# Attention and two MLPs on one core: key loads ahead of the branch in a shared tile, weights decoded through PSUM in wider blocks, and a new schedule

## The chip, the cores and the metric

One NeuronCore of one Trainium2 chip runs the whole program. The metric is the device time of one execution in microseconds; the kernel before takes 1524.06 us (median of 3 runs, 1523.6 to 1525.9).

## What is computed

```python
# attention: q [1,12288,128], kv [1,384,32,128], w_sr [128,128]
kv_pool = kv.reshape(B, H//4, 4, W//4, 4, C).mean(axis=(2, 4))   # 768 keys, 16 rows each
k = v = kv_pool.reshape(B, -1, C) @ w_sr
s = scale * (q @ k.T); a = exp(s - s.max(-1)); a /= a.sum(-1) + 1e-9
x = a @ v                                    # tokens x 128
# first MLP (2048 wide)
x = relu(x @ w_in)**2 @ w_out
# second MLP (2048 wide): a rational function of h
h = x @ w_in
P = a0 + a1*h + a2*h**2 + a3*h**3
Q = 1 + |b0|*|h| + |b1|*h**2
out = (P / (Q + 1e-6)) @ w_out
```

The weights of the MLPs arrive as float64, two 32-bit words each.

## The kernel before

The tokens lie along the free dimension and are cut into blocks: one of 384, then blocks of 512, then 384 and 256. A float32 product on TensorE is done either as one fp32 product (two instructions) or as three fp32r products of a high and a low part (high x high, high x low, low x high).

Before anything else DVE computes some 25 small coefficients from the six numbers a and b, and a flag, which all engines read. `tc.If` then takes one of two bodies of the same `program`: SQUARES, where the polynomial can be completed to a square, or TERMS. The trace shows SQUARES (line 921 and 923 run), so TERMS is not spoken of.

A planner (`Plan`) gets every piece of work with a priority, the engines that may do it (each with a cost and a penalty added to the priority), what it reads and writes, and the ring of buffers (`bufs`) or the PSUM bank (`caps`, eight banks in all) that it needs. It simulates the engines and writes out one order; each engine executes its instructions in that order, and semaphores hold an instruction until its data and buffers are ready. The dictionary SQUARES holds ring sizes, penalties and offsets of the priorities.

The stages, with their lines:

- Start: 16 loads of 48 keys (384 KB each, line 448) into the ring `e` of five tiles; DVE sums each over 16 rows (452). TensorE multiplies the halves of the sums by w_sr for the keys (477) and the values (492); ACT and DVE split the results (481, 485, 504, 507, 511).
- Weights: `decode` (line 521 on) loads a piece of 256 columns as pairs of words into a slot of Z (531), POOL squares the high word as a float (538) for a test of magnitude, and DVE builds the float32 in four steps in a tile K in SBUF: shift (541), or (546), or (551), and a select and multiply (556). ACT and POOL then make the high (572, 598) and low parts (575, 601) where a weight is used split. There are 32 pieces: eight each for w_in and w_out of two MLPs.
- Attention, per tile of 128 tokens: scores (642), minimum of the negated scores on DVE (646), exponential on ACT (649), reciprocal on DVE (656, 657), scaling on POOL (660); then transpositions (683), copies out of PSUM (687 to 703), products with the values (712 to 716).
- First MLP, per block of 512 tokens 16 pieces of 128 hidden units: three fp32r products (768 to 770), relu on ACT (810) or DVE (813), square on ACT (816) or POOL (819); ten of 16 pieces are split into gH on ACT (828) and gL on POOL (834) for three products with w_out (786 to 788), six use fp32 (782).
- Second MLP, per block eight pairs of pieces (`G` = 2): products (768 to 770), |h| on ACT (907), the denominator either as a square on ACT (915) or, for the pairs in `qpool`, as two steps on POOL (910, 912); the completed square on ACT (921) and the cubic on DVE (923); logarithm and exponential on ACT (932, 933); division with one Newton step on DVE (945, 947, 950); then the product with w_out as fp32 (782), or, for the pairs in `spl`, split by a cast on ACT or DVE (960, 961) and a remainder on POOL (963) into three fp32r products.

The three MLP and attention stages of different blocks run at the same time: the first MLP about 17.5 sixteenths of a block ahead of the second, attention 18 more.

Of the kernel before, what the change touches and what calls it, by code (L numbers as in the profile page):

```python
# [10 lines left out]
F32 = mybir.dt.float32  # L11
# [33 lines left out]
    d2=3,  # L45
    g=2,
    pair=('kk', 'qp', 'sq2', 'ln', 'y0', 'g0', 'tt', 'rr', 'g2', 'ml'),
    rem=[],
    md_act=1,
    md_dve=0.5,  # L50
    rl_act=0.5,
    rl_dve=0,
    qh_act=8,
    qh_dve=0,
    spd=[],
    spl=[3],
    qpool=[0, 3, 4, 7],
    sq_act=2,
    sq_pool=4,
    gh_act=0,  # L60
    gh_dve=60,
    mh_act=4,
    mh_dve=8,
    ml_pool=0,
    ml_dve=60,
    ev_dve=0.5,
# [4 lines left out]
    warm=0,  # L71
# [3 lines left out]
        mh2=-245.5, mh1=-25.5, sc=-10.25, tr=0.5, nr=-177.0, g2=-51.5, ex=-83.25, kk=-203.75, rl=1.5, tt=11.75,  # L75
        ev=65.0, mo2=10.25, ln=64.75, g0=-54.25, ab=-12.0, sq=182.75, y0=-12.25, mn=-121.5, qp=23.75, av=-39.5,
        mo1=4.25, sP=113.25, sq2=158.25, rr=90.25, mh=-26.5, ml=-114.0,
# [10 lines left out]
    hs=[1, 4, 7],  # L88
    lo_dve=60.0,
    bufs=dict(  # L90
        qr=2, qh=2, ql=2, e=5, mn=4, sm=8, aT=2, xh=2, xl=2, yh=2, yl=2, aH=2, aL=2, g1=8, U=3, K=2,
        Z=8, o=1, gH=2, gL=2, mH=1, mL=1,
    ),
    caps=dict(
        h2=2, yb=2, sc=4, st=3, x=1, h1=2, y1=1, y2=1,
    ),
    lead1=22.5,
    leada=14.0,
    d1=5,
    d2=4,  # L100
    g=2,
    pair=('kk', 'qp', 'ln', 'y0', 'g0', 'tt', 'g2'),
    rem=[],
    md_act=0,
    md_dve=8,
    rl_act=0,
    rl_dve=8,
    qh_act=0,
    qh_dve=60,
# [3 lines left out]
    sq_act=0,  # L113
    sq_pool=0.5,
    gh_act=0,
    gh_dve=60.0,
    mh_act=0,
    mh_dve=60.0,
    ml_pool=0,
    ml_dve=60.0,  # L120
    ev_dve=60.0,
    hi_dve=60.0,
    rg=2,
    low=6,
# [5 lines left out]
        mh2=-10.75, mh1=-2.0, sc=-2.75, tr=-1.5, nr=-7.75, g2=0.5, ex=4.5, z2=6.0, t1=-1.0, kk=3.5, rl=-0.5,  # L130
        tt=6.75, ev=-1.75, mo2=5.75, ln=8.75, g0=10.0, ab=-2.0, sq=11.5, y0=-2.75, mn=1.25, qp=-6.5, av=0.5,
        mo1=0.75,
    ),
    free=150.0,
)
# [49 lines left out]
class Plan:  # L185


    def __init__(self, cfg, banks=8):
        bufs, caps = cfg["bufs"], cfg["caps"]
        self.cfg = cfg  # L190
        self.bufs = bufs
        self.banks = banks
        self.caps = caps
        self.slot = {}
        self.ops = []
        self.keys = {}
        self.seq = {}
# [939 lines left out]
```

## Time and profile before

| | |
|---|---|
| median of 3 runs | 1524.06 us |
| the profiled execution | 1524.5 us |
| its span, first to last instruction | 1522.7 us |
| TensorE (PE) busy | 1454.4 us, 96% |
| VectorE (DVE) | 1414.5 us, 93% |
| ScalarE (ACT) | 1407.9 us, 92% |
| GpSimd (POOL) | 1169.0 us, 77% |
| loaded from HBM | 21.04 MB |

All shares are over the whole span; the stages differ. PE busy time includes modelled ends of matmuls that overlap, so the mean duration of one is longer than the distance to the next. PEclk, the granted clock, is 1.00 at 2.4 GHz and 0.50 at 1.2 GHz.

### The profile page before, as it was taken

How to read it: one execution, taken by the hardware profiler on the slowest of the kernel's cores; microseconds unless marked ns; L12 is line 12 of the kernel's file. 1: busy time of each engine (PE TensorE's matmuls, PEld its weight loads, DVE VectorE, ACT ScalarE, POOL GpSimd, SP SyncE). 2: the span in 40 equal slices, each digit the busy share in tenths (PEclk: the TensorE clock that was granted, in tenths of full speed). 3: DMA queues.
4: the chain of work that ended last, by engine and by line, in shares of the span. 5: the costliest groups of instructions: out<-in, count | busy, mean ns of one | idle time of the engine just before them, and what ended most of it. 6: DMA issues, size and time to landing. Idle time of an engine off the chain costs nothing.

```text
span 1522.7 us, 18759 instructions
## 1 busy us (share of the span) xinstructions
PE 1454.4 (96%) x5893; PEld 1038.7 (68%) x5893; DVE 1414.5 (93%) x1892; ACT 1407.9 (92%) x2339; POOL 1169.0 (77%) x962
## 2 busy tenths in 40 slices
PE   2788999999999999999999999999999999999996
PEld 2666776676767766776777677677767677767764
DVE  6999899999999998989899999899999989999997
ACT  1676999999999999999999999999999999999996
POOL 1877887967879967877977878778768768778662
PEclk9999999999999999999999999999999999999997
DMA  6221000000000000000000000000000000000000
GB/s 234 77 77 42 1 13 8 7 15 8 8 8 15 8 8 14 2 13 8 15 8 8 14 8 8 15 8 8 15 7 8 8 13 4 8 8 1 8 8 12
DMA packets 16701, 28.62 MB, mean 19 GB/s; under 512 B 1872, under 2 KB 6864, under 8 KB 16592
## 3 DMA queue, kind: packets, MB, share of 16 engines
q1 hardware_dynamic: 16592, 27.34, 5.5%
q8 instruction: 48, 0.79, 0.2%
q14 instruction: 61, 0.50, 0.1%
HBM read 21.04 MB, written 6.29 MB: 18 GB/s over the span
## 4 chain that ended last, share of the span: by engine, by line
PE 81%; DVE 9%; ACT 3%; issue 2%; POOL 1%; DVEq 0%; ACTq 0%; POOLq 0%
PE psum L782 24%; PE psum L768 11%; PE psum L770 10%; PE psum L769 10%; PE psum L642 5%; PE psum L787 4%; PE psum L788 4%; PE psum L786 4%; PE psum L683 3%; PE psum L713 2%; PE psum L714 2%; PE psum L712 1%; DVE K L546 1%; PE psum L716 1%; DVE psum L947 1%
## 5 line engine op out<-in xcount | busy, mean ns | idle before, releaser
L834 POOL TENSOR_TENSOR gL<-g,gH 128x512 fp32r<-128x512 f32 (+2 forms) x250 | 312.4, 1260 | 79.1 <-ACT gH L828 33.0
L782 PE MATMUL psum<-Z,w1o 128*128 128x512 f32 (+2 forms) x700 | 330.6, 583 | 4.9 <-DVE Z L950 4.3
L819 POOL TENSOR_TENSOR g<-g 128x512 f32<-128x512 f32 (+2 forms) x281 | 282.2, 1020 | 28.5 <-ACT g L810 16.2
L923 DVE SCALAR_TENSOR_TENSOR Z<-Z,cf,psum 128x512 f32<-128x512 f32 (+2 forms) x400 | 280.4, 719 | 19.0 <-ACT Z L921 16.7
L921 ACT ACTIVATE Z<-psum,cf 128x512 f32<-128x512 f32 (+2 forms) x400 | 275.6, 726 | 0.0
L945 DVE SCALAR_TENSOR_TENSOR Z<-Z,v,psum 128x1024 f32<-128x1024 f32 (+2 forms) x200 | 246.0, 1233 | 28.0 <-ACT psum L933 25.9
L907 ACT ACTIVATE U<-psum 128x512 f32<-128x512 f32 (+2 forms) x400 | 236.3, 625 | 20.9 <-PE psum L770 17.0
L947 DVE SCALAR_TENSOR_TENSOR psum<-K,cf,psum 128x1024 f32<-128x1024 f32 (+2 forms) x200 | 247.3, 1237 | 0.0
L950 DVE SCALAR_TENSOR_TENSOR Z<-psum,Z 128x1024 f32<-128x1024 f32 (+2 forms) x200 | 234.8, 1174 | 2.5
L932 ACT ACTIVATE U<-K,cf 128x1024 f32<-128x1024 f32 (+2 forms) x200 | 233.5, 1170 | 1.5 <-POOL K L912 1.3
L912 POOL TENSOR_TENSOR K<-K,U 128x1024 f32<-128x1024 f32 (+2 forms) x100 | 231.2, 2312 | 4.0
L910 POOL TENSOR_SCALAR K<-U,cf 128x1024 f32<-128x1024 f32 (+2 forms) x100 | 109.3, 1093 | 138.4 <-ACT U L907 83.1
L933 ACT ACTIVATE psum<-U 128x1024 f32<-128x1024 f32 (+2 forms) x200 | 208.8, 1049 | 1.3 <-DVE Z L950 0.5
L768 PE MATMUL psum<-yh,w1h 128*128 128x512 f32 (+2 forms) x400 | 191.4, 479 | 4.2 <-DVE Z L950 1.5
L768 PE MATMUL psum<-xh,w0h 128*128 128x512 f32 (+2 forms) x400 | 185.6, 464 | 3.2 <-DVE Z L950 1.1
L782 PEld LDWEIGHTS psum<-Z,w1o 128*128 128x128 f32 x700 | 130.0, 192 | 80.2 <-issue 57.0
L828 ACT ACTIVATE gH<-g 128x512 fp32r<-128x512 f32 (+2 forms) x250 | 158.6, 671 | 0.3 <-PE psum L788 0.2
L810 ACT ACTIVATE g<-psum 128x512 f32<-128x512 f32 (+2 forms) x252 | 151.8, 633 | 3.2 <-PE psum L770 2.2
L770 PE MATMUL psum<-yh,w1l 128*128 128x512 f32 (+2 forms) x400 | 154.3, 386 | 0.0
L769 PE MATMUL psum<-yl,w1h 128*128 128x512 f32 (+2 forms) x400 | 153.9, 385 | 0.0
L770 PE MATMUL psum<-xh,w0l 128*128 128x512 f32 (+2 forms) x400 | 153.6, 384 | 0.0
L769 PE MATMUL psum<-xl,w0h 128*128 128x512 f32 (+2 forms) x400 | 153.0, 383 | 0.0
(123 smaller groups left out, 3107.4 us busy)
## 6 DMA issues: line engine op xcount, KB each, us to landing
e<-in_kv_dram SPq DMA_DIRECT2D x16, 384.0 KB, 4.5
qr<-in_q_dram SPq DMA_DIRECT2D x22, 256.0 KB, 2.6
out_dram<-o SPq DMA_DIRECT2D x22, 256.0 KB, 2.0
Z<-in_moe_w_in_dram SPq DMA_DIRECT2D x16, 256.0 KB, 3.1
Z<-in_moe_w_out_dram SPq DMA_DIRECT2D x16, 256.0 KB, 2.6
qr<-in_q_dram SPq DMA_DIRECT2D x2, 192.0 KB, 3.8
out_dram<-o SPq DMA_DIRECT2D x2, 192.0 KB, 1.9
qr<-in_q_dram SPq DMA_DIRECT2D x1, 128.0 KB, 2.0
```

The lines of the kernel that those rows point to most:

```text
L768: nc.tensor.matmul(out=out, lhsT=w_hi[m][:, sl], rhs=hi, start=True, stop=False)
L769: nc.tensor.matmul(out=out, lhsT=w_hi[m][:, sl], rhs=lo, start=False, stop=False)
L770: nc.tensor.matmul(out=out, lhsT=w_lo[m][:, sl], rhs=hi, start=False, stop=True)
L782: nc.tensor.matmul(out=o, lhsT=w_o[m][:, place[m][fi], :], rhs=rhs(), start=first, stop=last)
L819: nc.gpsimd.tensor_tensor(out=G(), in0=G(), in1=G(), op=ALU.mult)
L834: nc.gpsimd.tensor_tensor(out=mk("gL", gl)[:, :T], in0=G(), in1=f(tiles[gh][:, :T]), op=ALU.subtract)
L907: one("ab", ACT, c_actp, lambda v: act(out=v(uu), in_=v(hh), func=AF.Abs), "U", [hh])
L921: one("sP", ACT, ptr(c_actp), lambda v: act(out=v(zz), in_=v(hh), func=AF.Square, bias=co["c"]), "Z", [hh])
L923: one("z3", DVE, ptr(c_dve), lambda v: stt(out=v(zz), in0=v(zz), scalar=co["nd"], in1=v(hh), op0=ALU.subtract, op1=ALU.mult), None, [hh], ...
L945: one("g0", DVE, ptr(c_dve), lambda v: stt(out=v(zz), in0=v(zz), scalar=e0, in1=v(yy), op0=ALU.add, op1=ALU.mult), None, [yy], [zz])
L947: one("tt", DVE, c_dl, lambda v: stt(out=v(yy), in0=v(ku), scalar=dl, in1=v(yy), op0=ALU.add, op1=ALU.mult), None, [ku], [yy])
L950: one("g2", DVE, c_dve, lambda v: stt(out=v(g_), in0=v(yy), scalar=2.0, in1=v(zz), op0=ALU.subtract, op1=ALU.mult, reverse0=True), None, [ ...
```

## The change

- One tile, `room`, is made before the branch, and so is wsr. The loads of w_sr and of all 16 key pieces are issued there, each into its own part of `room` (16 x 768 floats a partition). Inside, the reductions read from `room`. The fp32 rings Z, U, K, g1, aT, e, o and qr are cut from the same tile; `Plan.hold` makes the first user of a slot wait for the reductions of the keys that lay there. o and qr lie behind the keys.
- `decode` gets its width as an argument: 512 columns for w_in (four pieces instead of eight for each MLP), 256 as before for w_out. The three integer steps now write into a PSUM bank (`dc`, one bank) and the fourth writes the float32 into K or the weight tile. The square of the high word may run on ACT (penalty 0.5) instead of POOL. The planner's costs of the steps are those of plain DVE instructions.
- `warm=60`: 60 products of the identity with itself at the lowest priority, at the start. The identity is made first.
- `spl` becomes [0, 3]: one more pair of the second MLP is split. `qpool` becomes [0, 1, 3, 4, 6, 7]: two more pairs' denominators are made on POOL. `mh`, the cast for a split pair, takes both halves in one instruction.
- Ring sizes, penalties and all priority offsets are new.

```diff
 SQUARES = dict(
     bufs=dict(
-        qr=1, qh=1, ql=2, e=5, mn=11, sm=14, aT=2, xh=1, xl=2, yh=2, yl=2, aH=2, aL=3, g1=8, U=2, K=2, Z=6, o=1,
-        gH=5, gL=4, mH=1, mL=1,
+        qr=1, qh=1, ql=1, e=4, mn=14, sm=16, aT=1, xh=1, xl=1, yh=2, yl=2, aH=2, aL=2, g1=8, U=2, K=4, Z=7, o=1,
+        gH=6, gL=3, mH=1, mL=1,
     ),
-        h2=3, yb=4, sc=5, st=6, x=1, h1=5, y1=1, y2=1,
+        h2=3, yb=6, sc=6, st=6, x=1, h1=5, y1=1, y2=1, dc=1,
-    rl_act=0.5,
-    rl_dve=0,
+    rl_act=0,
+    rl_dve=2,
-    spl=[3],
-    qpool=[0, 3, 4, 7],
-    sq_act=2,
-    sq_pool=4,
+    spl=[0, 3],
+    qpool=[0, 1, 3, 4, 6, 7],
+    sq_act=0,
+    sq_pool=2,
-    mh_act=4,
-    mh_dve=8,
-    ml_pool=0,
+    mh_act=1,
+    mh_dve=0.5,
+    ml_pool=4,
-    warm=0,
+    warm=60,
...
+KC = 48
+
+RINGS = dict(Z=1024, U=1024, K=1024, g1=512, aT=512, e=768, o=768, qr=512)
...
+            for before in self.hold.get((tag, n), ()):
+                deps.update(self.keys[before]["w"])
...
+        if tag in RINGS:
+            n = turn[tag] = turn.get(tag, -1) + 1
+            at = ring_at[tag] + n % bufs[tag] * RINGS[tag]
+            t = room[:, at:at + RINGS[tag]]
...
     for c in range(0, NKEY, KC):
-        def go(c=c):
-            t = mk("e", ("kv", c), [128, KC, R2])
-            nc.sync.dma_start(out=t, in_=kvT[:, c:c + KC, :])
...
-        dma(P0, KC * R2 * 512, go, new=[("e", ("kv", c))])
+        dma(P0, KC * R2 * 512, lambda: None, new=[("const", ("kv", c))])
...
-            t = tiles["pool"][:, 0:128]
-            nc.tensor.matmul(out=o[:, 0:128], lhsT=t, rhs=t, start=True, stop=True)
+            nc.tensor.matmul(out=o[:, 0:128], lhsT=ident, rhs=ident, start=True, stop=True)
...
         def a1():
-            nc.vector.tensor_scalar(out=mk("K", da, [128, CW], I32), in0=hi(), scalar1=3, scalar2=0x3FFFFFF8,
+            mk("dc", dc)
+            nc.vector.tensor_scalar(out=word(), in0=hi(), scalar1=3, scalar2=0x3FFFFFF8,
                                     op0=ALU.logical_shift_left, op1=ALU.bitwise_and)
+        def word():
+            return tiles[dc][:, 0:CW].bitcast(I32)
...
-        P.op(prio, (POOL, c_pool(CW) + 110.0, m, 0), new=[("U", dm)], rd=[raw])
-        P.op(prio, (DVE, c_dve2(CW) - 150, a1, 0), new=[("K", da)], rd=[raw])
-        P.op(prio, (DVE, c_dves(CW), a2, 0), rd=[raw], wr=[da])
-        P.op(prio, (DVE, c_dve(CW), a3, 0), rd=[raw], wr=[da])
-        P.op(prio, (DVE, c_dve(CW), a4, 0), new=new, rd=[dm], wr=[da])
+        P.op(prio, [(POOL, c_pool(CW), m, 0), (ACT, c_acts(CW), m_a, 0.5)], new=[("U", dm)], rd=[raw])
+        P.op(prio, (DVE, c_dve(CW), a1, 0), new=[("dc", dc)], rd=[raw])
+        P.op(prio, (DVE, c_dve(CW), a2, 0), rd=[raw], wr=[dc])
+        P.op(prio, (DVE, c_dve(CW), a3, 0), rd=[raw], wr=[dc])
+        P.op(prio, (DVE, c_dve(CW), a4, 0), new=new + ([("K", da)] if dst is None else []), rd=[dm, dc])
...
+    nc.sync.dma_start(out=wsr, in_=w_sr)
+    n = KC * kvT.shape[2]
+    for c in range(kvT.shape[1] // KC):
+        nc.sync.dma_start(out=room[:, c * n:(c + 1) * n].rearrange("p (k r) -> p k r", k=KC),
+                          in_=kvT[:, c * KC:(c + 1) * KC, :])
```

## Rows read from the trace of the kernel before

**Rows 1.** Busy time by stretch: busy us and instructions per engine, granted clock, DMA share, GB/s.

```profile
core 0: us, PE busy (x) PEld busy (x) DVE busy (x) ACT busy (x) POOL busy (x), PEclk, DMA share, GB/s
0.00:20.00 20.00, 0.00 (x0) 0.00 (x0) 10.99 (x39) 1.28 (x1) 0.71 (x6) 1.00 0.59 195
20.00:40.00 20.00, 11.11 (x38) 8.61 (x38) 17.44 (x32) 6.31 (x14) 7.45 (x9) 1.00 0.72 252
30.00:160.00 130.00, 107.39 (x477) 83.64 (x477) 123.24 (x227) 86.90 (x185) 101.72 (x108) 0.95 0.22 71
200.00:1400.00 1200.00, 1198.71 (x4793) 845.55 (x4792) 1127.22 (x1419) 1169.98 (x1875) 960.23 (x748) 1.00 0.03 9
1480.00:1523.00 43.00, 27.72 (x105) 19.12 (x104) 33.66 (x55) 30.49 (x65) 11.91 (x11) 0.80 0.03 10
```

**Rows 2.** SP's queue in order of time: start us, us; two output stores, 15 blocks apart.

```profile
364.73 0.34 SPq L987 DMA_DIRECT2D out_dram<-o  x1
1253.55 0.34 SPq L987 DMA_DIRECT2D out_dram<-o  x1
```

**Rows 3.** Instructions in order of time, the first 30 us: start us, us, engine.

```profile
6.85 0.21 POOL masks.py:197 MEMSET ident<- 128x128 f32 x1 [6.41 <-DVE r L1073]
7.12 2.24 SPq L448 DMA_DIRECT2D e<-in_kv_dram  x5
7.75 0.15 DVE L1047 TENSOR_SCALAR cf<-cf 128x1 f32<-128x1 f32 x1
13.87 2.95 DVE L452 TENSOR_REDUCE o<-e 128x48 f32<-128x768 f32 x3 [1.46 <-DMA e<-in_kv_dram]
21.54 1.49 PE L492 MATMUL psum<-wsr,o 128*128 128x128 f32 x6
28.65 0.95 DVE L452 TENSOR_REDUCE o<-e 128x48 f32<-128x768 f32 x1 [0.82 <-DMA e<-in_kv_dram]
29.66 1.65 PE L477 MATMUL psum<-o,wsr 128*128 128x384 f32 x2 [6.63 <-DVE o L452]
```

**Rows 4.** Busy time by stretch, the first products and a later stretch.

```profile
20.00:22.00 2.00, 1.90 (x5) 1.30 (x6) 1.68 (x3) 0.22 (x1) 0.00 (x0) 1.00 0.95 349
52.00:54.00 2.00, 1.57 (x5) 1.57 (x6) 1.55 (x5) 1.15 (x5) 1.68 (x3) 0.50 0.34 117
```

**Rows 5.** DVE's instructions that write or read K, 30 to 160 us: busy us.

```profile
30.00:160.00 130.00, 80.62 (x129) 0.95 0.22 71
```

**Rows 6.** Two decode steps by line: duration ns least/median/greatest, first and last start us.

```profile
L546 DVE SCALAR_TENSOR_TENSOR K<-Z,K x32: 407/677/1514, 31.2 to 148.1; 128x256 int32<-128x256 int32 x32
L541 DVE TENSOR_SCALAR K<-Z x32: 276/648/1379, 30.7 to 146.6; 128x256 int32<-128x256 int32 x32
```

**Rows 7.** Groups by line, DVE, 200 to 1400 us: busy us, mean ns, idle before.

```profile
L813 DVE TENSOR_SCALAR g<-psum 128x512 f32<-128x512 f32 x118 | 79.6, 684 | 9.4 <-PE psum L770 7.4 <-POOL K L910 0.7 <-POOL mL L963 0.5
L947 DVE SCALAR_TENSOR_TENSOR psum<-K,cf,psum 128x1024 f32<-128x1024 f32 x167 | 213.6, 1279 | 0.0
```

**Rows 8.** The chain that ended last, in order of time, one fp32 piece.

```profile
593.11 3.43 PE psum L782 x8
```

**Rows 9.** TensorE in order of time, fp32r products; four more stand between these.

```profile
605.61 0.39 PE L768 MATMUL psum<-yh,w1h 128*128 128x512 f32 x1
...
606.97 0.39 PE L712 MATMUL psum<-aH,v_hi 128*128 128x512 f32 x1
```

**Rows 10.** Groups by line, POOL and ACT, 200 to 1400 us.

```profile
L819 POOL TENSOR_TENSOR g<-g 128x512 f32<-128x512 f32 x238 | 247.0, 1053 | 23.2 <-ACT g L810 13.9 <-DVE g L813 6.1 <-DVE sm L656 0.4
L912 POOL TENSOR_TENSOR K<-K,U 128x1024 f32<-128x1024 f32 x83 | 199.4, 2402 | 3.2
L910 POOL TENSOR_SCALAR K<-U,cf 128x1024 f32<-128x1024 f32 x83 | 93.6, 1127 | 102.2 <-ACT U L907 52.8 <-DVE psum L947 25.0 <-ACT Z L921 17.5
L963 POOL TENSOR_TENSOR mL<-Z,mH 128x1024 fp32r<-128x1024 f32 x21 | 50.4, 2398 | 5.4 <-ACT e L649 2.9 <-DVE mH L961 0.9 <-DVE mn L646 0.6
...
L915 ACT ACTIVATE K<-U,cf 128x1024 f32<-128x1024 f32 x83 | 100.3, 1208 | 0.0
...
L816 ACT ACTIVATE g<-g 128x512 f32<-128x512 f32 x80 | 52.5, 676 | 0.1
```

More of the change, by code (lines that the diff above doesn't have):

```diff
@@ L112 @@
     qpool=[],
[L113 to L122, printed above, removed]
+    sq_act=4,
+    sq_pool=2,
+    gh_act=0.5,
+    gh_dve=60,
+    mh_act=1,
+    mh_dve=8,
+    ml_pool=8,
+    ml_dve=0.5,
+    ev_dve=60,
+    hi_dve=1,
     rg=2,
-    low=6,
+    low=4,
     avs=4,
@@ L194, in __init__ @@
         self.slot = {}
+        self.hold = {}
         self.ops = []
@@ L359, in order, with program @@
         return sorted(start.values(), key=lambda x: x[:2])
-def program(ctx, tc, CFG, fast, co, qT, kvT, w_sr, w1_in, w1_out, w2_in, w2_out, outT):
+def program(ctx, tc, CFG, fast, co, room, wsr, qT, kvT, w1_in, w1_out, w2_in, w2_out, outT):
     nc = tc.nc
@@ L393, in program @@
     tiles = {}
+    turn, ring_at, at = {}, {}, 0
+    for t in [x for x in RINGS if x not in ("o", "qr")] + ["o", "qr"]:
+        at = max(at, NKEY * R2) if t == "o" else at
+        ring_at[t] = at
+        at += RINGS[t] * bufs[t]
+    assert at <= room_size(CFG)
     def mk(tag, key, shape=None, dtype=None):
@@ L398, in mk @@
             return tiles[key]
+        if tag in RINGS:
+            n = turn[tag] = turn.get(tag, -1) + 1
+            at = ring_at[tag] + n % bufs[tag] * RINGS[tag]
+            t = room[:, at:at + RINGS[tag]]
+            if dtype:
+                t = t.bitcast(dtype)
+            if shape:
+                size = 1
+                for x in shape[1:]:
+                    size *= x
+                t = t[:, 0:size]
+            else:
+                shape = big.get(tag, [128, TM])
+            if len(shape) == 3:
+                t = t.rearrange("p (a b) -> p a b", b=shape[2])
+            tiles[key] = t
+            return t
         t = pools[tag].tile(shape or big.get(tag, [128, TM]), dtype or dts.get(tag, F32), tag=tag, name=tag)
@@ L423, in program @@
     P = Plan(CFG)
+    for t in RINGS:
+        for n in range(bufs[t]):
+            x = ring_at[t] + n * RINGS[t]
+            P.hold[t, n] = [("poolT", c) for c in range(0, NKEY, KC) if c * R2 < x + RINGS[t] and x < (c + KC) * R2]
     def f(t):
@@ L470, in program @@
         P.op(1e6, (PE, c_mm4(128), warm(i), 0), new=[("st", "warm")] if i == 0 else [],
-             rd=["pool"] + [("poolT", c) for c in range(0, 384, KC)], wr=["warm"] if i else [])
+             rd=["ident"], wr=["warm"] if i else [])
     for h in range(2):
@@ L590, in load_w_out @@
                 decode(prio, key, words, w_o[m][:, p:p + n, :].rearrange("p k n -> p (k n)"),
-                       [("const", ("wo", m, fi)) for fi in range(c, c + n)])
+                       [("const", ("wo", m, fi)) for fi in range(c, c + n)], CW)
                 continue
-            decode(prio, key, words, None, [])
+            decode(prio, key, words, None, [], CW)
             p = HS[m].index(c)
@@ L1012, in program, with room_size @@
             emit()
+def room_size(cfg):
+    n = {t: w * cfg["bufs"][t] for t, w in RINGS.items()}
+    return max(sum(n.values()), 768 * 16 + n["o"] + n["qr"])
 @with_exitstack
@@ L1036, in attn_moe_moe @@
     pool = ctx.enter_context(tc.tile_pool(name="coef", bufs=1))
+    wsr = pool.tile([128, w_sr.shape[1]], F32, name="wsr")
+    room = pool.tile([128, max(room_size(SQUARES), room_size(TERMS))], F32, name="room")
     col = lambda n, name: pool.tile([128, n], F32, name=name)
@@ L1087, in attn_moe_moe @@
     V.memset(c1(co_g, 6), QC)
-    args = (qT, kvT, w_sr, w1_in, w1_out, w2_in, w2_out, outT)
+    args = (room, wsr, qT, kvT, w1_in, w1_out, w2_in, w2_out, outT)
     with tc.If(fits > 0) as branch:
```

103 lines of the change are left out of this document (50 added, 53 removed).

## The prediction

> **What bounds the kernel now.** I read the busy time by stretch first, then the order of time at the start, the groups by line, and the chain of waits. The stretches say where TensorE sets the time: from 200 to 1400 us it is busy 1198.71 of 1200, with ACT at 1169.98, DVE at 1127.22 and POOL at 960.23 [rows 1]. TensorE bounds, ACT is close behind, and POOL alone has room. Outputs leave at 364.73 and, 15 blocks later, at 1253.55 [rows 2], so a block of 512 tokens takes 59.25 us, and those 1200 us hold 20.25 blocks. The time that is not TensorE's lies at the two ends. No product runs before 20 us; from 20 to 40 TensorE idles 8.9; from 30 to 160 it is busy 107.39 of 130 at a granted clock of 0.95, while DVE is busy 123.24; in the last 43 us it is busy 27.72, with DVE at 33.66 and ACT at 30.49 [rows 1]. Three prices are wanted: the start, the ramp in which DVE decodes the weights, and the length of a block.
>
> Every sum is made against the profiled run, 1524.5 us, which is its span of 1522.7 plus 1.8; the median of the three runs, 1524.06, is 0.4 lower.
>
> **Key loads ahead of the branch.** Now SP's first key load issues at 7.12, after the flag; the queue is then full, with a DMA share of 0.95 at 349 GB/s [rows 3, 4]. The last reduction starts at 28.65 and the second key product at 29.66 [rows 3]. After the change all 16 loads have their own place, so nothing holds an issue back. At 0.45 us each (five took 2.24) [rows 3] they last from about 2.1, behind three small loads, to 9.3, so SP comes to its branch some 2 us later than now; the query load that follows lands behind the keys. 6.29 MB at 350 GB/s need 18 us: landed at 21.5, counted from 3.5, when the first can start to arrive. DVE still computes its coefficients first, to 7.9; 16 reductions 0.93 apart (three took 2.95) [rows 3] then end at 22.8, and the first half's two remainders, some 0.55 each, put the second product near 24. That is DVE's time, not the DMA's. Gain 29.66 - 24 = **5.6**. Other end: if the branch itself waits for the loads, DVE starts at 21.5 and ends at 36.4, so 6.9 are lost. POOL works inside the branch at 6.85, while DVE still computes coefficients until 7.9 [rows 3]; entry waits for the flag only, as far as this shows, so I take the gain. The rings' new waits (a weight load until the reductions over its part of the room are done) end by 23, and what they hold on SP, the next weight and query loads, would then still be behind the keys on the DMA engines.
>
> **Identity products at first.** 60 fp32 products of 128 columns; six such took 1.49 us [rows 3], so 60 take 15 at most and lie between 7.5 and 22.5, when TensorE has nothing to do. The first key product may start at 22 instead of 16; scores want the second. Cost 0; at half clock 30 us, to 37.5, so 13 late. Do they bring anything? From 20 to 22 us the granted clock is 1.00, the 2.4 GHz level, with no product before it; 0.50, the 1.2 GHz level, is granted at 52 to 54 [rows 4]. I take 0. The Trainium skill (TensorE: Matmul & The Clock Gate, What's actually happening) calls the throttled level the default, from which activity releases. By that the identity products would spare the first key and value products a half-rate run, 3 us of them here; the row of 20 to 22 us says otherwise for this kernel.
>
> **Decode through PSUM, wider.** The 32 pieces of 256 columns have four DVE steps each; with one other instruction (1 us) they keep DVE busy 80.62 us of the 130 [rows 5]. The second step takes 0.407 at least and 1.514 at most for one and the same shape, the first 0.276 and 1.379 [rows 6]: they wait inside for something, and POOL is busy 101.72 of the 130 us beside them [rows 1]. Steps with an operand in PSUM show no such spread: 0.684 for 512 columns, 1.279 for 1024, on average, beside a POOL as busy [rows 7]. So I price the new steps at 0.69 for 512 columns and 0.41 for 256: eight pieces at 4 x 0.69 and sixteen at 4 x 0.41 make 22.1 + 26.2 = 48 us, and DVE is spared 80 - 48 = **32 us** of the 123 that it works in the ramp. Against it: the first step's least, 0.276, is below any PSUM row and goes to 0.41. The Trainium skill has the rule (VectorE: DVE Perf Modes, Why PSUM operands drop a tier): an operand in PSUM costs the doubled rate. By it the first step alone grows by 32 x 0.13 = 4 us; its median of 0.648 shows that the doubled rate is not what it gets here.
>
> What of the 32 us reaches the end? TensorE idles 22.6 us in the ramp and loses to the clock about 5: together 28, the most that can come back. The least is 0, if TensorE waits for the attention chain (scores, maximum, exponential, scaling on POOL, transposition) all the same. What is late next is POOL with 101.72; at DVE's present share, 95%, it needs 107, 23 less than 130. ACT may now take the magnitude squares off it. I take the middle, **15**. The PSUM bank that decode takes from eight for some 48 us could cost an eighth of them, 6; it stays in the range.
>
> **One more split pair.** Two of a block's products with w_out in the second MLP go from fp32 to three fp32r products each. Eight fp32 instructions, which are four products, take 3.43 us in the chain: 0.858 a product [rows 8]. Six fp32r products run from 605.61 to 606.97: 0.227 each, 0.68 for three [rows 9]. 2 x 0.178 x 24.375 blocks (12480/512) = **8.7** less, all on TensorE. Its price: a cast of two halves (nearest row: 0.676 on ACT) and a remainder of 2.40 on POOL [rows 10].
>
> **Two more pairs' denominators on POOL.** ACT loses two squares of 1.21 a block; POOL gains 2 x (1.127 + 2.402) = 7.06 and that remainder [rows 10]. POOL's 960.23/20.25 = 47.4 a block become 56.9, of a block of 59.25 - 0.36 = 58.9. That is 97%, as full as ACT is now; it must give up squares of the first MLP (11.75 a block at 1.053) [rows 10] to ACT, which takes 0.676 for one and has 2.4 - 1.4 = 1.0 freed. All three together have room: (960 + 1170 + 1127)/20.25 = 160.8, plus 9.5 - 2.4 + 1.4, make 169.3 of 176.7. TensorE idles 0.1% now; with less room elsewhere I put **+4** on it, between 0 and the first rival below. Other buffers, penalties and offsets reorder the same work; rings grow (K, Z, gH) and shrink (e, aL, ql): 0, with 5 either way. In the last 43 us DVE and ACT bound; two fewer squares and one more cast a block: 0, with 3 either way.
>
> **The sum.** 1524.5 - 5.6 - 15 - 8.7 + 4 = 1499.2; less 0.4 for the median, **1499**.
>
> **Rivals.** *POOL sets the block* (slower). The first denominator step, which comes twice more, is also the one before which POOL idles most: 102.2 us before 83 of them, 1.23 each [rows 10]. Six of them, 7.4, and 56.9 make 64.3; three squares given to ACT leave 61.1, 2.2 over 58.9, times 20.25 = 45 in place of the 4: 1540. It decides from a block of 60.3 us on (the gains, 29.3, over 20.25 blocks). Against it: these are the waits of an engine with room, and more squares can move. 14%.
> *The ramp stays as long* although DVE is freed, because the attention chain and POOL hold it: 1514. For it: POOL is busy 78% of that stretch too. 12%.
> *The ramp gives back all 28 and the fuller POOL costs nothing*: 1499 - 13 - 4 = 1482. 15%.
> *The branch waits for the loads*, so that the change doesn't do what it says: 5.6 + 6.9 more, 1511.5. 5%.
> A mild form of the first with the second meets at no change: 4%. My forecast, within 8 us of 1499, has the other 50%.
>
> **How the numbers follow.** Two parts in ten lie outside 1481 to 1517: the slow rival, the case of no change and a little of the fast one. A measurement can tell about 0.2%, 3 us, from no change. Faster: 50 + 12 + 15 + 5 = 82%; same 4%; slower 14%.
>
> **What would show it.** Right: the second key product near 24; decode steps near 0.69 and 0.41 with little spread; the last second step well before 148; outputs 58.9 apart; POOL near 95% busy between 200 and 1400. Wrong: DVE's first reduction only after 20 us; TensorE as idle as now from 30 to 160, with DVE idle too; gaps before POOL's denominator steps as long as now, and outputs over 60 us apart.

## The result, and the profile after

The changed kernel takes **1506.23 us** (median, 1505.8 to 1507.04), the kernel before beside it 1523.83 us (1521.9 to 1525.9): a ratio of 0.9885, 95% interval 0.9868 to 0.9902. That is 17.6 us less, about 1.2%. The forecast was 25 us less, 1499. The profiled execution has a span of 1504.3 us against 1522.7.

Busy time by stretch in the changed kernel, with the columns of [rows 1] (the last stretch ends, as there, with the span):

```profile
0.00:20.00 20.00, 11.87 (x90) 11.87 (x91) 12.11 (x41) 1.28 (x1) 0.70 (x6) 1.00 0.82 302
20.00:40.00 20.00, 12.12 (x66) 10.74 (x65) 13.91 (x23) 7.66 (x16) 3.84 (x4) 0.83 0.56 197
30.00:160.00 130.00, 122.87 (x581) 101.28 (x582) 119.52 (x232) 112.06 (x230) 110.27 (x102) 0.96 0.18 57
200.00:1400.00 1200.00, 1190.10 (x4818) 847.02 (x4817) 1121.38 (x1396) 1167.46 (x1894) 1093.34 (x796) 1.00 0.03 9
1461.00:1504.00 43.00, 30.26 (x111) 21.00 (x111) 34.49 (x56) 31.22 (x66) 19.98 (x19) 0.80 0.03 10
```

Against [rows 1]: from 30 to 160 us TensorE is busy 122.87 instead of 107.39. From 200 to 1400 it is busy 1190.10 instead of 1198.71, while GpSimd went from 960.23 to 1093.34 and ScalarE stayed where it was, at 97%. The output stores that answer to [rows 2] stand in SyncE's queue so:

```profile
344.39 0.34 SPq L1016 DMA_DIRECT2D out_dram<-room  x1
...
1239.68 0.34 SPq L1016 DMA_DIRECT2D out_dram<-room  x1
```

The first is 20.3 us earlier than in [rows 2], the second, 15 blocks later, only 13.9. A block takes 59.69 us, not 59.25. So the change gains at the ramp and pays some of it back, block by block.

Busy times overlap and hide the clock, so I kept a ledger of TensorE alone. Each product gets the shortest distance at which the middle of the traces shows it repeated: 0.429 us for an fp32 instruction of 512 columns (3.43 for eight, [rows 8]), 0.227 for an fp32r product of 512 ([rows 9]), 0.178 for one of 384, 0.109 for a transposition, nothing for an identity product. The sum over a kernel is its work; a stretch less the work in it is TensorE's lost time, whether idle or at a lower clock. An instruction that lies across the edge of a stretch was counted on both sides, so the work stands some 4 to 5 us too high here and the losses, taken together, as much too low. Counted once each, the work is 1403.5 us before and 1395.1 after and the loss from 160 to 1400 us 21.0 and 36.5; the differences between kernels, on which the readings rest, move by less than 1 us. The kernel without identity products (next section), whose order is that of the changed one, loses 36.6 there by this count.

```
us lost by TensorE         span    work   0:30 30:160 160:1400 rest
before                    1522.7  1408.6  27.8   37.2    18.9  30.3
after                     1504.3  1399.7  28.1   13.1    34.6  28.9
after less before          -18.4    -8.9  +0.3  -24.1   +15.7  -1.4
```

These terms make up the 18.4 us. The start, the first 30 us, gave nothing; the ramp gave 24.1 and the second split pair 8.9 (8.4 when each instruction is counted once); the end, after 1400 us, gave 1.4; the middle took 15.7 back.

### The profile page after: what moved, and what is told of

It is laid out like the page before. It is cut to its first block, busy times and chain, and to the rows that moved or that the text cites. A ratio compares the mean times of both kernels' runs of the same rounds, so it can differ in the third digit from the quotient of the medians.

```text
span 1504.3 us, 18834 instructions
## 1 busy us (share of the span) xinstructions
PE 1457.4 (97%) x6063; PEld 1057.8 (70%) x6063; DVE 1388.8 (92%) x1848; ACT 1413.7 (94%) x2371; POOL 1314.7 (87%) x995
## 4 chain that ended last, share of the span: by engine, by line
PE 64%; POOL 13%; ACT 12%; DVE 7%; issue 3%; DMA 0%; POOLq 0%; SPq 0%; ACTq 0%; DVEq 0%
PE psum L811 16%; PE psum L797 8%; PE psum L798 8%; PE psum L799 8%; PE psum L671 5%; POOL room L941 4%; PE psum L815 3%; PE psum L816 3%; PE psum L817 3%; PE psum L712 3%; POOL gL L863 2%; POOL room L939 2%; ACT room L950 2%; ACT room L961 2%; ACT room L936 2%
## 5 line engine op out<-in xcount | busy, mean ns | idle before, releaser
L941 POOL TENSOR_TENSOR room<-room 128x1024 f32<-128x1024 f32 (+2 forms) x150 | 347.3, 2316 | 3.0
L863 POOL TENSOR_TENSOR gL<-room,gH 128x512 fp32r<-128x512 f32 (+2 forms) x250 | 311.9, 1260 | 8.9 <-PE psum L816 2.6
L952 DVE SCALAR_TENSOR_TENSOR room<-room,cf,psum 128x512 f32<-128x512 f32 (+2 forms) x400 | 281.0, 719 | 16.5 <-ACT room L950 14.4
L811 PE MATMUL psum<-room,w1o 128*128 128x512 f32 (+2 forms) x600 | 288.8, 587 | 4.4 <-DVE room L979 4.4
L974 DVE SCALAR_TENSOR_TENSOR room<-room,v,psum 128x1024 f32<-128x1024 f32 (+2 forms) x200 | 246.3, 1233 | 29.7 <-ACT psum L962 27.8
L950 ACT ACTIVATE room<-psum,cf 128x512 f32<-128x512 f32 (+2 forms) x400 | 271.9, 709 | 0.0
L976 DVE SCALAR_TENSOR_TENSOR psum<-room,cf,psum 128x1024 f32<-128x1024 f32 (+2 forms) x200 | 247.3, 1237 | 0.0
L961 ACT ACTIVATE room<-room,cf 128x1024 f32<-128x1024 f32 (+2 forms) x200 | 229.2, 1148 | 17.9 <-POOL room L941 17.0
L979 DVE SCALAR_TENSOR_TENSOR room<-psum,room 128x1024 f32<-128x1024 f32 (+2 forms) x200 | 235.0, 1175 | 2.9
L936 ACT ACTIVATE room<-psum 128x512 f32<-128x512 f32 (+2 forms) x400 | 228.5, 608 | 6.1 <-PE psum L799 4.3
L839 ACT ACTIVATE room<-psum 128x512 f32<-128x512 f32 (+2 forms) x272 | 161.6, 619 | 3.5 <-PE psum L799 3.1
```

Source lines behind the costliest of these rows:

```text
L811: nc.tensor.matmul(out=o, lhsT=w_o[m][:, place[m][fi], :], rhs=rhs(), start=first, stop=last)
L863: nc.gpsimd.tensor_tensor(out=mk("gL", gl)[:, :T], in0=G(), in1=f(tiles[gh][:, :T]), op=ALU.subtract)
L936: one("ab", ACT, c_actp, lambda v: act(out=v(uu), in_=v(hh), func=AF.Abs), "U", [hh])
L941: one("qp", POOL, c_pool, lambda v: nc.gpsimd.tensor_tensor(out=v(ku), in0=v(ku), in1=v(uu), op=ALU.mult), None, [uu], [ku])
L950: one("sP", ACT, ptr(c_actp), lambda v: act(out=v(zz), in_=v(hh), func=AF.Square, bias=co["c"]), "Z", [hh])
L952: one("z3", DVE, ptr(c_dve), lambda v: stt(out=v(zz), in0=v(zz), scalar=co["nd"], in1=v(hh), op0=ALU.subtract, op1=ALU.mult), None, [hh], ...
```

## The start: what held the second key product

Instructions of the changed kernel in order of time (start, duration, engine):

```profile
2.11 12.21 SPq L1083 DMA_DIRECT2D room<-in_kv_dram  x16
...
8.13 14.77 PE L489 MATMUL psum<-ident 128*128 128x128 f32 x114 [8.13 <-POOL ident masks.py:199]
...
9.20 8.69 DVE L480 TENSOR_REDUCE room<-room 128x48 f32<-128x768 f32 x10 [0.65 <-DVE cf L1089]
...
22.73 0.81 PE L499 MATMUL psum<-room,wsr 128*128 128x384 f32 x2
...
24.17 0.56 DVE L507 SCALAR_TENSOR_TENSOR k_lo<-psum,k_hi 128x384 fp32r<-128x384 f32 x1 [6.28 <-ACT k_hi L503]
...
30.40 1.65 PE L499 MATMUL psum<-room,wsr 128*128 128x384 f32 x2 [5.52 <-DVE room L480]
```

The loads are issued from 2.11 to 14.32, at 0.76 us each and not the 0.45 of the forecast. DVE's first reduction starts at 9.20, 4.7 us before that of [rows 3] and before the last load is issued; the branch did not wait for the loads to land. Then DVE stands idle for 6.28 us. Its queue holds the first half's remainder (line 507) ahead of the last six reductions, that remainder needs the first key product, and TensorE runs identity products from 8.13 to 22.9, ahead of it in its own queue. The second key product comes at 30.40, not 24, and later than the 29.66 of [rows 3].

**Identity products left out.** In the changed kernel, with the planned order unchanged, 59 of the 60 are not issued.

```diff
     def warm(i):
         def go():
-            o = mk("st", "warm") if i == 0 else tiles["warm"]
+            if i:
+                return
+            o = mk("st", "warm")
```

> The changed kernel with its order of work kept, but 59 of the 60 identity products left out (their results are used nowhere). Theory: they hold TensorE until 22.6 us, the first key product waits behind them, DVE waits 6.28 us for the first half's remainder with six reductions queued behind it, and the second key product comes at 30.4. Without them it comes near 24 and the time falls by 5 to 8 us, to 1498 to 1501. Rival A: the start is covered by something later (weights, scaling on POOL), and the time stays within 2 us of 1506. Rival B: without them the clock is lower in the first 40 us, and the time rises.

Measured: 1500.81 us (1500.19 to 1501.48), ratio to before 0.986 [0.9844, 0.9877], 5.4 us faster than the changed kernel. The same instructions in its trace:

```profile
16.31 1.65 PE L501 MATMUL psum<-room,wsr 128*128 128x384 f32 x2 [7.31 <-DVE room L480]
...
18.58 0.56 DVE L509 SCALAR_TENSOR_TENSOR k_lo<-psum,k_hi 128x384 fp32r<-128x384 f32 x1 [0.60 <-ACT k_hi L505]
...
24.82 1.65 PE L501 MATMUL psum<-room,wsr 128*128 128x384 f32 x2 [5.58 <-DVE room L480]
```

DVE idles 0.60 us instead of 6.28 and the second key product starts at 24.82, close to where the forecast's arithmetic had put it (24). The theory of the expectation held; neither rival did. The lost time goes from 28.1 to 24.4 in the first 30 us and from 10.9 to 8.3 from 30 to 60 (ledger). Part of the latter is clock. Here are 30 to 35 us in the changed kernel, and then in the one without identity products:

```profile
30.00:35.00 5.00, 4.60 (x14) 3.99 (x15) 3.82 (x7) 1.04 (x3) 0.00 (x0) 0.50 0.47 152
```

```profile
30.00:35.00 5.00, 1.90 (x11) 1.39 (x9) 4.78 (x13) 3.99 (x9) 2.85 (x3) 1.00 0.20 68
```

The identity products end before 25 us, TensorE idles 5.5 us, and the granted clock is 0.50 just when the second half's products and the first scores run.

## The ramp: decode through PSUM

The second and the first integer step in the changed kernel (count: shortest, median, longest in ns; first and last start), to be read against [rows 6]:

```profile
L574 DVE SCALAR_TENSOR_TENSOR psum<-room,psum x24: 411/428/696, 31.0 to 114.7; 128x256 int32<-128x256 int32 x16, 128x512 int32<-128x512 int32 x8
L566 DVE TENSOR_SCALAR psum<-room x24: 411/421/689, 30.3 to 114.1; 128x256 int32<-128x256 int32 x16, 128x512 int32<-128x512 int32 x8
```

The spread within one shape is gone: 0.407 to 1.514 us before, 0.411 to 0.441 now for 256 columns and 0.672 to 0.696 for 512. The prices of the forecast, 0.41 and 0.69, are met, and all decode steps together take 48.8 us of DVE. The last second step starts at 114.7 instead of 148.1.

**Decode through PSUM alone.** The kernel before, its pieces still 256 columns wide, with the three integer steps in one PSUM bank (`dc=1`). A piece takes its slot of K only at the fourth step then, and the planner's costs of the four steps are those of the changed kernel, so the order of the work is another one too.

```diff
-            nc.vector.tensor_scalar(out=mk("K", da, [128, CW], I32), in0=hi(), ...
+            mk("dc", dc)
+            nc.vector.tensor_scalar(out=word(), in0=hi(), ...   # word(): the PSUM bank
...
-            t = tiles[da]
+            t = word()
```

> The kernel before with one edit: the three integer steps of the decode write into a PSUM bank, at the width of 256 as before. Theory: a step is 0.41 to 0.42 us instead of 0.6 to 0.8, DVE is spared some 30 us before 150 us, and the time falls by 15 to 22 us, to 1502 to 1509. Rival: the ramp shortened through the wider pieces, the earlier weight loads or the new order, and this edit alone gives less than 6 us.

Measured: 1523.22 us, ratio 1.0002 [0.9992, 1.0011], no change; 1502 to 1509 had been expected. Its stretches, 30 to 160 and 200 to 1400 us:

```profile
30.00:160.00 130.00, 119.57 (x557) 98.49 (x556) 117.17 (x256) 107.25 (x222) 112.74 (x126) 0.94 0.24 70
200.00:1400.00 1200.00, 1192.51 (x4772) 844.80 (x4771) 1110.14 (x1402) 1166.75 (x1873) 931.08 (x725) 1.00 0.03 9
```

The ramp does what was forecast: TensorE is busy 119.57 of 130 us there, the loss falls from 37.2 to 18.1, and the fourth output leaves at 346.45 instead of 364.73. Then 11.0 us more than before are lost in the middle and 7.3 after 1400 us, with the same products, a GpSimd that does less than before and a ScalarE as full. A gain at the ramp does not carry to the end by itself.

**Decode back in SBUF.** The changed kernel with the three integer steps in a slot of K again; widths and all else as changed.

```diff
-            mk("dc", dc)
+            mk("K", da, [128, CW])
...
-            return tiles[dc][:, 0:CW].bitcast(I32)
+            return tiles[da].bitcast(I32)
```

> The changed kernel with the integer steps of the decode writing into K in SBUF again, widths kept. Theory: the steps take 1.2 to 1.6 us for 512 columns beside a busy POOL, DVE has 30 us more before 160 us, and the time rises by 10 to 20 us, to 1516 to 1526. Rival: the ramp does not hang on these steps now that the pieces are wider and ACT takes squares: within 4 us of 1506.

Measured: 1551.53 us, ratio 1.0185 [1.0168, 1.0202], 45 us slower than the changed kernel and far above the 1516 to 1526 expected. Groups by line, DVE from 20 to 160 us and TensorE from 60 to 100 us (busy us, mean ns, idle before):

```profile
L579 DVE SCALAR_TENSOR_TENSOR room<-room 128x512 int32<-128x512 int32 x8 | 8.0, 994 | 0.0
L574 DVE SCALAR_TENSOR_TENSOR room<-room 128x256 int32<-128x256 int32 x16 | 8.1, 507 | 0.0
...
L742 PE MATMUL psum<-aL,v_hi 128*128 128x384 f32 x3 | 1.5, 515 | 23.9 <-DVE aL L732 23.9
```

The wide third step takes 994 ns on average where the changed kernel's takes 686. The average hides two kinds: of its eight, the shortest takes 679 ns, the middle ones 680, the longest 1760. All decode steps sum to 60 us instead of 48.8, so their length explains 11 of the 45 us. The larger part is order. Between 60 and 100 us DVE runs decode steps nearly without a break, and one product with the values waits 23.9 us for a remainder (732) queued behind them; in that stretch TensorE is busy 9.04 of 40, at a granted clock of 0.51. Without the PSUM bank, of which `dc=1` lets one piece be open at a time, K's four slots let the plan put the pieces close together; the order is seen, that reason for it is only argued. So the 45 us are not the price of SBUF operands alone, and this run does not part the two.

What makes a step long stands in the order of time. Here is one of the run above, with GpSimd's instruction beside it:

```profile
46.63 1.73 POOL L604 TENSOR_TENSOR w0l<-room,w0h 128x512 fp32r<-128x512 f32 x1
47.15 1.75 DVE L574 SCALAR_TENSOR_TENSOR room<-room 128x512 int32<-128x512 int32 x1
```

GpSimd's instruction is running when VectorE's starts and ends at 48.36; VectorE's ends 0.55 us later. All long steps are like this one. In the kernel before, 62 of the 128 decode steps are over 15% longer than an undisturbed one (0.276 us for the first step, 0.41 for the others). All 62 start while a GpSimd instruction runs; the first steps end 0.15 us after it, the others 0.27 to 0.29. Of the 66 short ones 14 start beside one too, but in its first 0.22 or its last 0.15 us. In the changed kernel 77 of the 96 steps start beside a running GpSimd instruction too, and none is long. The Trainium skill (SBUF — State Buffer, SBUF: two separate sides) says that a VectorE operation in a two-port mode, or one with two SBUF inputs against a GpSimd operation that reads SBUF, and a GpSimd operation exclude each other for a whole instruction. The trace agrees; the first step has one SBUF input and waits like the others (276 to 1379 ns in [rows 6]), so two SBUF inputs are not the only case here.

## The middle: where the gain was given back

**Four pairs' denominators on GpSimd, two split pairs.**

```diff
-    qpool=[0, 1, 3, 4, 6, 7],
+    qpool=[0, 3, 4, 7],
```

> The changed kernel with four pairs' denominators on POOL again (0, 3, 4, 7) instead of six. Theory: a block takes 59.7 us where TensorE's work is 58.2, because POOL is 91% busy and its denominators come late; with 7 us less on POOL a block shortens by 0.4 to 0.8, and the time falls by 8 to 16 us, to 1490 to 1498. Rival: ACT, which gets two squares of 1.2 us a block back, is the bound; a block grows and the time rises to 1512 or more.

Measured: 1509.47 us, ratio 0.9919 [0.9902, 0.9935]. GpSimd's busy time from 200 to 1400 us falls from 1093.34 to 1011.84, yet the middle still loses 34.8 us. The theory that GpSimd was merely too full (1490 to 1498 us) fell in that form: what GpSimd was spared went to ScalarE, which is at 1171.36 there. The rival, 1512 or more, was not met either.

**Four pairs on GpSimd, one split pair**, as before the change; and **six pairs, one split pair**.

```diff
-    spl=[0, 3],
-    qpool=[0, 1, 3, 4, 6, 7],
+    spl=[3],
+    qpool=[0, 3, 4, 7],
```

> The changed kernel with four pairs on POOL and one split pair, as the kernel before has them. Theory of a late POOL: the block is that of before, 59.25, with TensorE's 0.35 a block back: 1506 - 10 = 1496, and no better than four pairs with the second split pair. Rival, ACT as the bound: between 1506 and 1515, since the cast of the second split pair also leaves ACT. Rival, the offsets alone make the block longer: 1506 + 8 = 1514.

```diff
-    spl=[0, 3],
+    spl=[3],
```

> The changed kernel with one split pair instead of two, six pairs' denominators on POOL kept. TensorE's work grows by 8.3 us; casts of 24 pairs leave ACT and DVE, remainders of 24 x 2.4 us leave POOL. Theory: with two split pairs the engines beside TensorE are too full, the middle loses 35 us of TensorE instead of 20, and one split pair gives 1506 + 8 - 14 = 1500. Rival: the middle stays at 35 because of the six pairs on POOL or the offsets: 1514.

Measured: 1506.93 us (ratio 0.9888 [0.9867, 0.9909]) and 1512.91 us (0.9922 [0.9906, 0.9939]).

```
us lost by TensorE             span    work   0:30 30:160 160:1400 rest
four pairs, one split         1505.4  1407.9  28.1   13.9    20.5  35.2
four pairs, two split         1507.1  1399.8  28.1   14.4    34.8  29.8
six pairs, one split          1511.2  1408.3  28.1   13.0    29.6  32.4
six pairs, two split (after)  1504.3  1399.7  28.1   13.1    34.6  28.9
```

The first lies in the range of ScalarE as the bound (1506 to 1515), the second near the rival of its expectation (1514). Neither list does it alone. With four pairs, the second split pair saves 8.1 us of work and costs 14.3 in the middle; with six it costs 5.0. With one split pair, the two more on GpSimd cost 9.1; with two they cost nothing.

**Another order of the same work.** The kernel before, the planner's time until a freed buffer may be used again raised, so that the order changes and the work doesn't.

```diff
-    free=150.0,
+    free=170.0,
```

> The kernel before with one number of the planner changed, the pause before a freed buffer is handed on (150 to 170): the same instructions in the same numbers, in another order from the first attention block on. The decode alone through PSUM won 19 us before 160 us and lost them again, 11 between 160 and 1400 and 7 after. Theory: the offsets of the kernel before fit its own order, and any other order costs some 10 to 20 us in the long middle and the tail: 1530 to 1545. Rival: an order is worth little, this one too, and the time is within 5 us of 1523; then the decode edit itself costs the middle.

Measured: 1535.93 us, ratio 1.0089 [1.0072, 1.0105]. The middle loses 18.7 us, as before; the ramp 46.7 instead of 37.2. An order alone is worth 12 us. The time lies in the expected range, 1530 to 1545, but not for the expected reason: this order costs the ramp, and the middle nothing. One order says little of another, though: in the run with decode through PSUM alone the middle loses 11 us more with the same products.

**The old dictionary on the new code.** The changed program with SQUARES of before and `dc=1` added: loads ahead, shared tile, decode through PSUM and wider, but no identity products and the old lists, penalties and offsets.

```diff
-    qr=1, qh=1, ql=1, e=4, mn=14, ...      warm=60,   spl=[0, 3],   ...
+    qr=1, qh=1, ql=2, e=5, mn=11, ...      warm=0,    spl=[3],      ...
```

> The changed code with the dictionary of the kernel before (rings, penalties, offsets, four pairs on POOL, one split pair, no identity products) and one bank for the decode: the early key loads and the decode through PSUM in wider pieces, without the new schedule. Theory: second key product near 24, 20 us won in the ramp, and 10 to 18 lost again to offsets that were made for another order: 1508 to 1514. Rival: the parts add up and it gives 1524 - 5.6 - 20 = 1498.

Measured: 1504.14 us (1500.2 to 1505.17), ratio 0.9869 [0.9851, 0.9886]: at least as fast as the whole change. The second key product is at 24.64, the start loses 23.5, the ramp 11.6, the middle 26.0, the rest 32.5 us. The new structure carries all of the gain; the new schedule with its identity products adds nothing to it.

**One step halved, on each of three engines.** What in the middle is late? Three kernels keep the changed kernel's order and take half of one step of the second squarer's chain away: ScalarE's logarithm (961), GpSimd's multiplication before it (941), or VectorE's step after it (976), each over 512 columns of its 1024. The other half is left out.

```diff
-            one("ln", ACT, ptr(c_acts), lambda v: act(out=v(uu), in_=v(ku), func=AF.Ln, bias=dl_ap), ...
+            one("ln", ACT, ptr(c_acts), lambda v: act(out=v(uu)[:, 0:1], in_=v(ku)[:, 0:1], func=AF.Ln, bias=dl_ap), ...
```

> The changed kernel, its plan and order as they are, but the logarithm of the second squarer's denominator (ScalarE, 165 instructions of 1184 ns from 200 to 1400 us) taken over one of its pair's two blocks of 512 only: half of that logarithm is left out. By the width-512 rows beside it (630 to 670 ns) this spares ScalarE about 165 x 0.53 = 87 us of its 1167 us of work in that stretch. Theory A (ScalarE at its ceiling, 97% busy in every kernel so far, is what TensorE's lost time in the middle follows): the 34.6 us that TensorE loses from 200 to 1400 us in the changed kernel fall to 12 or less, and the run comes out at 1478 to 1488 us. Theory B (the length of the chain from one product to the next, whichever engine): they fall too, but so they do in the next two runs. Theory C (the order in which the instructions are queued): 30 or more are left, 1500 to 1507 us.

```diff
-                out=v(ku), in0=v(ku), in1=v(uu), op=ALU.mult), None, [uu], [ku])
+                out=v(ku)[:, 0:1], in0=v(ku)[:, 0:1], in1=v(uu)[:, 0:1], op=ALU.mult), None, [uu], [ku])
```

> The changed kernel, plan and order as they are, but GpSimd's multiplication in the denominators of the second squarer (124 instructions of 2405 ns from 200 to 1400 us) done over one of the two blocks only: half of it is left out. That spares GpSimd about 124 x 1.2 = 149 us of its 1093 us there and shortens the same chain by 1.2 us, more than twice what the halved logarithm takes off. Theory A (ScalarE): nothing of the loss in the middle goes, 30 to 35 us are left, 1500 to 1507 us. Theory B (the chain's length): the loss falls the most of the three, to 10 or less, 1478 to 1485 us. Theory D (GpSimd after all, which the run with four pairs on GpSimd spoke against): as B here, but the halved step on VectorE does nothing.

```diff
-                out=v(yy), in0=v(ku), scalar=dl, in1=v(yy), op0=ALU.add, op1=ALU.mult), None, [ku], [yy])
+                out=v(yy)[:, 0:1], in0=v(ku)[:, 0:1], scalar=dl, in1=v(yy)[:, 0:1], op0=ALU.add, op1=ALU.mult), ...
```

> The changed kernel, plan and order as they are, but the step of VectorE that multiplies the denominator into the exponential's result (165 instructions of 1279 ns from 200 to 1400 us) done over one of the two blocks only: half of it is left out. That spares VectorE about 165 x 0.6 = 99 us of its 1121 us there and takes 0.6 us off the chain, as much as the halved logarithm. Theory A (ScalarE): 30 to 35 us stay lost in the middle, 1500 to 1507 us. Theory B (the chain's length): the loss falls as much as with the halved logarithm. If VectorE is what is late, only this run falls.

Measured: 1495.52, 1488.53 and 1506.49 us; ratios 0.9818 [0.9802, 0.9834], 0.9774 [0.9757, 0.979] and 0.9886 [0.9865, 0.9906].

```
                      mean of the step, ns    engine busy 200:1400   lost 160:1400
after                          -                      -                  34.6
logarithm, ACT            1184 ->  732         1167.46 -> 1124.86        25.1
product, POOL             2405 -> 1294         1093.34 ->  967.52        17.8
step after it, DVE        1279 ->  749         1121.38 -> 1048.90        33.9
```

VectorE's step takes 0.53 us off the same chain as the logarithm's 0.45, and changes nothing: it is not the chain's length that costs, and VectorE is not late, though it is 93% busy. Both ScalarE and GpSimd count. GpSimd's step gave more because more was taken away: 124 times 1.11 us, 138 in all, for 16.8 us less loss, against 165 times 0.45, 75 in all, for 9.5. That is 0.12 and 0.13 us for each us spared; VectorE's 87 us gave 0.7. Of the theories in the three expectations, A named ScalarE alone and expected nothing of GpSimd; it fell. B wanted all three to help; it fell too. C, the order alone, wanted none to, and fell. D, GpSimd, is right in part: ScalarE counts as well, and the loss did not fall to 10 or less. What they share stands in the groups by line (busy us, mean ns, then idle time of ScalarE before it and what ended it), from 200 to 1400 us: first the kernel before, then the changed one, then the one with GpSimd's product halved.

```profile
L932 ACT ACTIVATE U<-K,cf 128x1024 f32<-128x1024 f32 x166 | 199.7, 1206 | 0.4 <-POOL K L912 0.2
```

```profile
L961 ACT ACTIVATE room<-room,cf 128x1024 f32<-128x1024 f32 x165 | 194.9, 1184 | 13.2 <-POOL room L941 12.5
```

```profile
L961 ACT ACTIVATE room<-room,cf 128x1024 f32<-128x1024 f32 x168 | 203.8, 1215 | 0.1
```

Before, ScalarE hardly waited for GpSimd's denominators (0.4 us). Now it does, 13.2 us, though it had next to nothing to spare: it is busy 97% in both kernels. Its idle time as a whole is about the same, 30.0 us of the 1200 before and 32.5 after; what it waits for has changed. Before, most of it, 21.4 us, ended with a product of TensorE, which set the pace; now 8.3 do. Halving the product takes the wait for GpSimd away (0.1 us), ScalarE's busy time rises to 1179.91 in the same 1200 us, and the middle's loss falls to 17.8, about that of the kernel before (18.9). The length of this wait is no measure of the loss: with four pairs and two split it is 8.5 us and 34.8 are lost, with the halved logarithm 23.3 and 25.1 are lost.

GpSimd's side, where [rows 10] has 102.2 us idle before 83 first steps:

```profile
L939 POOL TENSOR_SCALAR room<-room,cf 128x1024 f32<-128x1024 f32 x124 | 139.8, 1127 | 57.8 <-ACT room L936 47.9
L941 POOL TENSOR_TENSOR room<-room 128x1024 f32<-128x1024 f32 x124 | 298.2, 2405 | 2.1
```

124 pairs instead of 83, 0.47 us idle before each instead of 1.23. The slack that let the product come in time is gone, and the two engines wait for each other: GpSimd 47.9 us for ScalarE's |h| (936), ScalarE 12.5 us for GpSimd's product. That the work of these two engines sets the middle's loss is shown by the halved steps; how much of the 15.7 us each part of the change brought there is not.

Two things stay open. The run with decode through PSUM alone loses 29.9 us in the middle, and the one with the old dictionary 26.0, with four pairs on GpSimd, one split pair and that wait small (0.4 and 3.3 us). So there is another way to lose some 10 us in the middle, which no run here parts from the order. And each of these runs has an order of its own except those with identity products left out or a step halved, so the table of lists above says what a list with its plan is worth, not what the list alone is.

**The best of both.** The changed kernel without identity products and with the lists of before.

```diff
-    spl=[0, 3],
-    qpool=[0, 1, 3, 4, 6, 7],
+    spl=[3],
+    qpool=[0, 3, 4, 7],
...
+            if i:
+                return
```

> The changed kernel without 59 of its 60 identity products (the plan still counts them) and with the lists of before: four pairs' denominators on GpSimd, one pair of the second squarer split. The start should give back 5.4 us as it did alone (1506.2 to 1500.8), on top of what the old lists gave: 1506.9 - 5.4 = 1501.5 if the two add. If start and middle are not independent (TensorE that starts earlier runs into ScalarE's ceiling sooner), 1505 to 1507 us. If the smaller load on ScalarE and GpSimd in the middle is what the earlier start needed to reach the end, 1495 to 1499 us and the fastest of all.

Measured: 1500.0 us (1497.94 to 1501.42), ratio 0.9842 [0.9826, 0.9859]. The two add up as expected (1501.5). It can't be told from the changed kernel without identity products (1500.81); both beat the change and the kernel before, and the smaller edit is the deletion of the identity products. Against the old dictionary on the new code (1504.14), which has the same lists and no identity products, the new offsets and rings may be worth some 4 us; the two intervals overlap.

## Why the prediction was right, and where it was not

**The time.** 1499 was forecast, 1506.23 measured, inside the range of 1481 to 1517, and faster as forecast. That it came within 7 us is in part luck, since terms that were wrong by 6 to 12 us cancel in the sum. Term by term, by the ledger:

- **Key loads ahead of the branch, 5.6 forecast: failed, +0.3 in the first 30 us.** The working of this term was right by itself: without identity products the second product starts at 24.82, 4.8 earlier than in [rows 3]. What failed is the step after it, "Cost 0" for the identity products. I wrote that the first key product may start at 22 "instead of 16; scores want the second", and had counted the first half's two remainders into DVE's time two sentences earlier. Those remainders need the first product, and six reductions queue behind them. A late first product thus makes the second one late, with DVE idle 6.28 us. What is queued behind a waiting instruction was not followed up for the very engine on which the term rested.
- **That they bring nothing: right, for a wrong reason.** I took the granted clock of 1.00 at 20 to 22 us [rows 4] for TensorE's real rate. The durations say otherwise. One key product, two instructions, takes 1.65 us in [rows 3], and 1.65 for the very first without identity products, but 0.81 right behind them: 1.65 was the half rate. By durations the rule that I set aside (the Trainium skill, TensorE: Matmul & The Clock Gate, What's actually happening: throttled is the default) agrees with the trace. It would have saved some 1.5 us on the first half's products (1.65 + 1.49 against 0.81 + 0.83); but they start 6 us later, and the second half's at 30.40 run at half rate again, after an idle stretch. The branch of my text at half clock ("to 37.5, so 13 late") did not come about: 120 instructions took 15.6 us. That they took about the 15 us I allowed was luck. The six instructions of 1.49 us in [rows 3] are three fp32 products and ran at the half rate, so at the price of that row 60 products take 30; I read instructions as products, and the rise of the rate at 12 us made it good.
- **Decode through PSUM, 15 forecast: right in mechanism, mis-sized; 24.1.** Steps of 0.42 and 0.69 us, a sum of 48.8 us against 48: as worked out. "I take the middle" of 0 to 28 was too timid. DVE was the late engine of the ramp, and once spared, little else took its place: the ramp's loss fell to 13.1, and from 60 to 160 us to 2.2. The run with decode through PSUM alone, 19.1 less there with the narrow pieces, shows that most of it is this edit; the rest is not parted between the wider pieces, the earlier start and the order. My upper end was also low: busy time with a correction for the clock gave 28, while the ledger finds 37.2 us lost there before.
- **One more split pair, 8.7 forecast: right, 8.9.** Its price lay elsewhere (14.3 or 5.0 us of the middle in the runs above).
- **Fuller GpSimd, 4 forecast: mis-sized, 15.7.** A block takes 59.69 us, not 58.9. The 4 was set between 0 and the first rival without a row of its own. I had named the waits before the denominator's first step and asked whether they recur, and they shrank; the new wait is at the other end of that step, ScalarE's logarithm behind GpSimd's product, and ScalarE was the engine with no room for it. Squares did move, as forecast: GpSimd is 91% busy, not 97%. A part of the 15.7 may be the open one above.
- **The tail, 0 with 3 either way: right, -1.4.**

The sum 5.6 + 15 + 8.7 - 4 = 25.3 has become -0.3 + 24.1 + 8.9 - 15.7 + 1.4 = 18.4: two errors of about 6 and 12 us against one of 9.

**The rivals.** The branch did not wait for the loads (first reduction at 9.20). The ramp did not stay as long; it gave back 24.1 of the 28 us that the fast rival counted on, but the fuller GpSimd was not free. GpSimd did not set the block alone at 61.1 us; the mechanism of the slow rival, work moved to GpSimd that makes blocks longer, is there at a third of its price, 15.7 of 45 us, and together with a ScalarE that had no room.

## What to carry to other kernels

Instructions that are to fill idle time stand in an in-order queue ahead of real work: before pricing them at nothing, follow the first result behind them into every other engine's queue, and see what is queued behind its reader there. A stage freed at one end gives only as much as the stages behind it can take; with three engines above 90%, move work only to where no full engine waits for its result. To find which of several full engines is late, keep the order, halve one step on each in turn, and divide what the time gives back by the work that was taken away.

## What the runs showed of the hardware

The granted clock of the first stretches is not TensorE's rate there. TensorE's instructions in stretches of 2 us, changed kernel, from the first identity product on (busy us and instructions, granted clock, DMA share, GB/s):

```profile
8.00:10.00 2.00, 1.87 (x9) 1.00 1.02 404
10.00:12.00 2.00, 2.00 (x11) 1.00 1.03 416
12.00:14.00 2.00, 2.00 (x20) 1.00 1.03 409
14.00:16.00 2.00, 2.00 (x20) 1.00 1.04 404
```

The count doubles at 12 us, from 9 to 11 instructions to 20, all with 1.00 granted by the profile. So the engine began at the 1.2 GHz level and rose while it ran identity products, and the row shows neither. Later the row and the durations do agree: at 0.50 from 30 to 35 us the two instructions of a key product take 1.65 us again. In early stretches, trust durations.

A VectorE step that meets a running GpSimd instruction can wait for its end inside its own duration, where no idle time shows it: the same step on the same 512 columns takes 679 to 1760 ns, 994 on average, with two operands in SBUF, and 677 to 696, 686 on average, with one of them in PSUM. The PSUM operand has a price in the first step, which has one input: undisturbed it takes 0.41 us for 512 columns in SBUF and 0.69 in PSUM.
